# Attention and two MLPs on one core: product order, a planner rule, load order and four zero products

## The chip, the cores and the metric

One core of a Trainium2 chip runs the whole kernel. The metric is the device time of one launch in microseconds; of several runs the median is taken. TensorE is called PE here, VectorE DVE, ScalarE ACT, GpSimd POOL and SyncE SP, as in the profile.

## The reference

The kernel computes a decayed linear attention over 2 batches, 8 heads, 768 positions and a head size of 64, and then two MLPs over the 1536 tokens. Each MLP has a width of 512 and an inner width of 2048:

```python
for b in range(nb):                              # blocks of 64 positions
    intra = (q_b @ k_b.T) * Dmask @ v_b          # Dmask = lam ** (i - j) below the diagonal
    inter = (q_b * lam_pow) @ kv_state
    out[b] = intra + inter
    kv_state = lam_block * kv_state + (k_b * rev_pow).T @ v_b
x = out as [1536, 512]
h = x @ w_in;  x = (h * tanh(softplus(h))) @ w_out
h = x @ w2_in; y = relu(h) ** 2 @ w2_out
```

All arrays are float32.

## The kernel before

**Arithmetic.** Every float32 operand of an MLP product is split into a high and a low part in a reduced type (`fp32r`): ACT writes the high part, DVE subtracts it from the raw value for the low part. Each product is then three PE matmuls (`mm3`, L295): high by low, low by high, high by high. The weights arrive as int64 words; ACT (`m`, L565), DVE (`t`, L570) and a join on DVE (`bits`, L577) make float32 of them.

**Attention.** The tokens come in twelve chunks of 128. A call `attention(j)` handles chunks 2j and 2j+1: PE makes the scores (`sc`, L424, 16 matmuls a chunk), DVE multiplies them by the decay mask (`a`), POOL scales the keys (`kd`) and the queries (`qd`), PE makes the state's update (`sd`, L447), the output from the scores (`xo`, L466) and from the state (`xo`, L475). The two chunks of a call share one `xo` tile and one `sd` tile in PSUM. When a call's `xo` is complete, ACT and DVE read it: for the first 512 tokens into a high part (`xh`), a low part (`xl`) and a raw copy (`xr`), for the others into the raw copy alone. Each chunk needs two loads of 512 KB, `qk` and `kv`.

**MLPs.** Each of the two layers `L` goes through four blocks `g` of 512 inner columns. The tokens are three tiles of 512: tile 0 is handled apart, tiles 1 and 2 are a pair. The pair's products up and down are formed by seven products of sums and differences instead of eight (`up_pair`, `down_pair`): a product is two PE steps of 12 matmuls each (names `P1...`, `Q1...`), and results are passed on from one PSUM tile to the next by an ACT copy (`seed`, `keep`), which later products accumulate onto. Tile 0's up product is plain (`up`) in four blocks; in the blocks of `OWN`, (0,2), (1,1), (1,2) and (1,3), it is made by seven products as well (`up_own`): products U1, U7, U6, U2, U5, U4, U3 of 12 matmuls each. Their four accumulators a, b, f and e lie in two PSUM tiles of two banks: a and b in `ua`, f and e in `ub`. U1 goes to a, ACT copies a to b, U7 goes to f and is kept, U6 goes onto a, U2 onto b; ACT then copies a to e and DVE adds f to a; U5 goes onto e, U4 onto a, U3 onto e. Results a, b, e go through the activation into SBUF.

`TURNED` names the blocks (0,3) and (1,3), in which the pair's products come before those of tile 0, and the pair's down products before tile 0's. In the other blocks tile 0 comes first.

**The planner.** The order of every engine's instructions is written by a list scheduler in the kernel (`Plan`). Each step (`op`) has an engine, an estimated time, the values that it reads and writes, and for PE a `rank`. In the plan PE takes the ready step of the lowest rank; the other engines take the ready step whose due time (`late`) comes first, which follows from the PE steps that need it. Values live in 51 SBUF units of 4 KB a partition or in four PSUM tiles of two banks; a step is only taken when its values have a place. The first twelve loads on SP have their order from the list `FIRST`. The planner's times are estimates; on the chip semaphores hold each instruction until what it depends on is done. The planner knows a dependency between steps by their keys, which may name a half of a PSUM tile, such as `(one, 1)`.

**What follows the order.** The main loop at the end calls, for each block, the weights, `up` or `up_own`, the pair's `up_pair`, `down` and `down_pair`, with ranks that rise by 100 from call to call. Before the first load has landed PE runs eight zero matmuls (`warm_up`, L339) on a tile of its own.

Of the kernel before, what the change touches and what calls it, by code (L numbers as in the profile page):

```python
# [20 lines left out]
P = 128  # L21
# [3 lines left out]
CH = 128  # L25
TB = 512
WARM = 8
GF = 4
STRETCH = 1.4
SPLIT = ((0, 0),)  # L30
# [11 lines left out]
OWN = ((0, 2), (1, 1), (1, 2), (1, 3))  # L42
# [6 lines left out]
class Val:  # L49


    def __init__(self, name, space="S", dtype=F32):
        self.name, self.space, self.dtype = name, space, dtype
        self.left, self.slot, self.tile, self.was = 0, None, None, None
        self.full = self.seeded = False


class Op:
# [7 lines left out]
class Plan:  # L66
# [67 lines left out]
    def run(self, start, units):  # L134
        self.dues(start)
        free = {"S": list(range(units)), "P": list(range(4))}
        clock = dict.fromkeys(self.LAG, 0.0)
        left = {o: len(o.before) for o in self.ops}
        ready = {e: [] for e in self.LAG}
        for o in self.ops:  # L140
            if not left[o]:
                o.at = 0.0
                ready[o.eng].append(o)
        releases, order, last, table = [], [], {}, None

        turn = {}
        for o in sorted((o for o in self.ops if o.eng == "PE"), key=lambda o: o.rank):
            for v in o.vals:
                if v.space == "P":
                    turn.setdefault(v)  # L150

        def fits(v):


            if v.space == "S":
                return free["S"]
            full = [s for s in free["P"] if s in last and last[s].full]
            return full if v.seeded else [s for s in free["P"] if s not in full] + full

        front = sorted((o for o in self.ops if o.eng == "PE"), key=lambda o: o.rank)  # L160
        now, n, drift = 0.0, 0, 0.0
        while n < len(self.ops):
            while releases and releases[0][0] <= now:
                _, v = releases.pop(0)
                free[v.space].append(v.slot)
            while front and front[0].start is not None:
                drift = max(0.0, front[0].start - front[0].late)
                front.pop(0)
            for e in ready:
                if clock[e] > now:  # L170
                    continue
                can = [o for o in ready[e] if o.at <= now and (e == "PE" or o.late + drift - now < o.ahead)]
                if not can:
                    continue
                best = None
                for o in sorted(can, key=lambda o: o.rank if e == "PE" else o.late + (
                        self.SWITCH[1] if o.table and o.table != table else 0.0)):
                    need = defaultdict(int)
                    for v in o.vals:
                        if v.slot is None:  # L180
                            need[v.space] += 1
                    if any(v.seeded and v.slot is None and not fits(v) for v in o.vals):
                        continue
                    if o.eng != "PE" and need["P"] and next(v for v in turn if v.slot is None) not in o.vals:
                        continue
                    if all(len(free[s]) >= k + (o.spare if s == "S" else 0) for s, k in need.items()):
                        best = o
                        break
                if best is None:
                    continue  # L190
                o = best

                if e != "PE" and any(q.at > now and q.at < now + 0.7 * o.us and q.late < o.late - 2.0
                                     for q in ready[e]):
                    continue
                for v in sorted((v for v in o.vals if v.slot is None), key=lambda v: v.name):
                    v.slot = fits(v)[0]
                    free[v.space].remove(v.slot)
                    if v.space == "P":
                        last[v.slot] = v  # L200
                o.start, o.end = now, now + o.us
                if o.table and o.table != table:
                    o.end, table = o.end + self.SWITCH[0], o.table
                clock[e] = o.end
                ready[e].remove(o)
                order.append(o)
                n += 1
                for v in o.vals:
                    v.left -= 1
                    v.was = max(v.was or 0.0, o.end + o.lag)  # L210
                    if not v.left:
                        bisect.insort(releases, (v.was, v), key=lambda r: r[0])
                for a in o.after:
                    left[a] -= 1
                    if not left[a]:
                        a.at = max(b.end + (b.lag if (b.eng != a.eng or b.lag > 1) and (b, a) not in self.orders else 0.0)
                                   for b in a.before)
                        ready[a.eng].append(a)
            times = [c for c in clock.values() if c > now]
            times += [o.at for r in ready.values() for o in r if o.at > now]  # L220
            times += [r[0] for r in releases[:1]]
            times += [o.late + drift - o.ahead + 1e-6 for e in ready if e != "PE" for o in ready[e]
                      if o.late + drift - o.ahead + 1e-6 > now]
            times = [t for t in times if t > now]
            if not times:
                stuck = [o.name for r in ready.values() for o in r][:20]
                held = sorted({v.name for o in self.ops for v in o.vals if v.slot is not None and v.left and v.space == "S"})
                raise RuntimeError(f"stuck {held} at {now} with {n} of {len(self.ops)}: {stuck} {len(free['S'])} {len(free['P'])}")
            now = min(times)
        self.order = order  # L230
        return order
# [3 lines left out]
def attention_mlps(ctx, tc, lam, qk, kv, w_in, w_out, w2_in, w2_out, out):  # L235
# [21 lines left out]


    FIRST = {n: 0.01 * i for i, n in enumerate(
        "qk0 st00000 kv0 st00001 qk1 kv1 qk2 kv2 st00010 st00011 qk3 kv3".split())}  # L260

    plan = Plan({"DVE": AHEAD, "ACT": AHEAD, "POOL": AHEAD, "SP": AHEAD})
    op = plan.op
# [136 lines left out]
    def attention(j):  # L400
# [14 lines left out]
        for n, c in enumerate(cs):  # L415
# [7 lines left out]
                        r = slice(e * D, (e + 1) * D)  # L423
                        nc.tensor.matmul(out=o[:, e, p], lhsT=t[r, 1, p], rhs=t[r, 0, p], start=True, stop=True)  # L424

            op("PE", 0.95, scores, [(q, "q"), (q, "k")], [(sc, 0)], name=sc.name, rank=rank + n)
            op("DVE", 1.3, lambda a=a, sc=sc: tt(tl(a, 2, NP, CH), tl(sc, 2, NP, CH), tl(mask, 2, NP, CH), ALU.mult),
               [(sc, 0), *masked], [(a, 0)], name=a.name)
            if not (last and n):
# [268 lines left out]
                    pair.append(v)  # L698
                own[L, kind, n] = tuple(pair)

    def up_own(L, g, rank):

        w = 2 * CH
        back = g >= HOME[L]
# [21 lines left out]
        def product(i, o, onto):  # L726
            lh, ll, left = stationary(L, g, 0, i)
            rh, rl, right = moving(i)

            def products():  # L730
                for s in range(2):
                    c = slice(s * P, (s + 1) * P)
                    q = bank(o)[:, s * w : (s + 1) * w]
                    for k in range(2):
                        mm3(q, left(lh)[:, k, c], left(ll)[:, k, c], right(rh)[:, k], right(rl)[:, k],
                            s == 0 and k == 0, k == 1, onto=onto, pieces=True)

            parts = range(2) if back else x_parts(L, 0) if i < 4 else (0,)
            reads = [(lh, 0), (ll, 0), *((v, j) for v in (rh, rl) for j in parts)] + ([o] if onto else [])
            op("PE", 1.44, products, reads, [o], name=f"U{i}{L}{g}", rank=rank + count[0])  # L740
            count[0] += 1

        def to(x, y, name):
# [125 lines left out]
        n = {5: 0, 6: 1, 7: 2, 3: 3}[i]  # L869
        return s_hi[L, g, kind, n // 2], s_lo[L, g, kind, n // 2], lambda v: tl(v, 2, 2, 2 * P)[:, n % 2]  # L870

    def up_pair(L, g, rank, rest=None):

        count = [0]

        def product(i, o=None):
# [8 lines left out]
            for s in range(2):  # L885
# [4 lines left out]
                            k == 0, k == 1, onto=onto)  # L890

                reads = [(x, 0) for x in (lh, ll, rh, rl)] + ([(o, s)] if onto else [])
                op("PE", 1.37, products, reads, [(o, s)], name=f"P{i}{L}{g}{s}", rank=(rest if rest and count[0] > 1 else rank) + count[0])
                count[0] += 1
            return o

# [217 lines left out]
    def ranks(n=100):  # L1114
        nonlocal rank
        rank += n
        return rank

    for L in range(2):
        for g in range(NG):  # L1120
# [4 lines left out]
            if (L, g) == (1, 0):  # L1125
                own_forms(1)
            turned = (L, g) in TURNED
            first = turned and ranks()
            if (L, g) in OWN:
                sums(L, g)  # L1130
                up_own(L, g, ranks())
            else:
                up(L, g, 0, ranks() if rank else UP)
            weights(L, g, 1, 0)
# [11 lines left out]
            if (L, g) in SPLIT:  # L1146
                opened, before = before, ranks()
                up_pair(L, g, opened, ranks())
            else:
                up_pair(L, g, first or ranks())  # L1150
            sums(L, g, 1)
# [57 lines left out]
```

## Time and profile before

| | us |
|---|---|
| median of 3 runs | 541.66 (541.22 to 542.62) |
| the profiled execution | 542.34 |
| its span, first to last instruction | 539.3 |
| PE busy | 527.2 (98%), 3358 matmuls |
| DVE busy | 428.1 (79%) |
| ACT busy | 400.7 (74%) |
| POOL busy | 32.1 (6%) |
| HBM traffic | 88.08 MB read, 26.21 MB written, 212 GB/s over the span |

The span is divided into stages. Attention fills the first 62 us, mixed with the first block's up product; the blocks of layer 0 go to about 350 us with parts of layer 1 begun between, and those of layer 1 to the end. A busy PE is not PE at its peak: a matmul's row covers its way through the engine, and the next one starts before it ends. In the rows a line of many matmuls is merged (`x24`), with its start, its length and, in brackets, the idle time ahead of it with what ended it. Block (1,2)'s own products begin at 412.88 us, for instance.

### The profile page before, as it was taken

The page shows a single profiled execution, that of the slowest core. Times are in us where ns is not written, and L with a number is a line of the kernel's source. Part 1 is how long each engine was busy: PE and PEld are TensorE (multiplying, and loading weights), DVE is VectorE, ACT ScalarE, POOL GpSimd, SP SyncE. Part 2 cuts the span into 40 slices and gives each one's busy share as a digit, 9 for nine tenths or more (in the row PEclk, how much of TensorE's full clock was granted, in tenths as well). Part 3 has the DMA queues.
Part 4 walks back from the last instruction along what each step waited for, and adds up shares of the span by engine and source line. Part 5 has one row for each costly group of instructions (what it writes and reads, how often), then busy time and mean ns, then how long its engine had stood idle before and what let it go on. Part 6 is the DMA issues. An engine that isn't in the chain of part 4 may idle for free.

```text
span 539.3 us, 8479 instructions
## 1 busy us (share of the span) xinstructions
PE 527.2 (98%) x3358; PEld 457.0 (85%) x3358; DVE 428.1 (79%) x465; ACT 400.7 (74%) x460; POOL 32.1 (6%) x32
## 2 busy tenths in 40 slices
PE   8899999999999899999999999999999999999997
PEld 5798888888888788888888888998899888988995
DVE  5897977976996579889898989976886777887862
ACT  3667658876887879787888787868777878866930
POOL 2675200000000000000000000000000000000000
PEclk9999999999999999999999999999999999999999
DMA  8998330399489862954130400399899814970033
GB/s 314 409 408 276 120 116 1 117 369 400 167 326 409 278 198 99 384 218 157 37 121 1 153 4 1 134 359 414 340 354 363 314 62 152 404 302 1 1 118 117
DMA packets 33353, 114.84 MB, mean 213 GB/s; under 512 B 3618, under 2 KB 5666, under 8 KB 33314
## 3 DMA queue, kind: packets, MB, share of 16 engines
q1 hardware_dynamic: 33312, 114.31, 57.4%
q8 instruction: 26, 0.43, 0.3%
q14 instruction: 13, 0.11, 0.1%
q10 hardware_dynamic: 2, 0.00, 0.0%
HBM read 88.08 MB, written 26.21 MB: 212 GB/s over the span
## 4 chain that ended last, share of the span: by engine, by line
PE 96%; DVE 2%; ACT 1%; issue 0%; ACTq 0%
PE p L300 16%; PE dn L300 16%; PE q L300 13%; PE e L300 10%; PE o L300 9%; PE up L300 8%; PE b L300 8%; PE ua L300 4%; PE ub L300 3%; PE sc L424 2%; PE xo L466 2%; PE sd L447 1%; PE xo L475 1%; PE warm L339 1%; DVE a L291 1%; ACT ub L288 0%
## 5 line engine op out<-in xcount | busy, mean ns | idle before, releaser
L291 DVE TENSOR_TENSOR sl<-s,sh 128x1024 fp32r<-128x1024 f32 x32 | 40.6, 1275 | 10.1 <-ACT sh L288 10.0
L565 ACT ACTIVATE m<-st 128x512 f32<-128x512 f32 (+1 forms) x66 | 42.1, 666 | 6.7 <-DMA st<-in_moe_w_in_dram 6.5
L577 DVE SCALAR_TENSOR_TENSOR t<-m,t 128x1024 int32<-128x1024 int32 x32 | 38.6, 1221 | 6.1 <-ACT m L565 5.9
L291 DVE TENSOR_TENSOR wl<-t,wh 128x1024 fp32r<-128x1024 f32 x32 | 38.8, 1221 | 1.8 <-ACT wh L288 1.3
L291 DVE TENSOR_TENSOR el<-D,eh 128x1024 fp32r<-128x1024 f32 x32 | 38.9, 1219 | 1.6 <-ACT eh L288 0.7
L288 ACT ACTIVATE sh<-s 128x1024 fp32r<-128x1024 f32 x32 | 33.4, 1051 | 3.7 <-DVE s L291 3.7
L288 ACT ACTIVATE wh<-t 128x1024 fp32r<-128x1024 f32 x32 | 33.4, 1051 | 1.7 <-DVE t L577 1.7
L288 ACT ACTIVATE eh<-D 128x1024 fp32r<-128x1024 f32 x32 | 32.9, 1051 | 1.2 <-DVE D L291 1.2
L291 DVE TENSOR_TENSOR el<-h,eh 128x1024 fp32r<-128x1024 f32 x24 | 29.3, 1220 | 1.8 <-ACT eh L288 1.3
L570 DVE TENSOR_SCALAR t<-st 128x512 int32<-128x512 int32 (+1 forms) x66 | 27.1, 444 | 3.5 <-PE p L300 2.1
L288 ACT ACTIVATE ap<-o 128x1024 f32<-128x1024 f32 x18 | 18.5, 1027 | 12.8 <-PE o L300 12.8
L291 DVE TENSOR_TENSOR D<-h,h 128x1024 f32<-128x1024 f32 x16 | 19.1, 1222 | 8.8 <-ACT h L809 6.1
L291 DVE TENSOR_TENSOR gl<-h,gh 128x1024 fp32r<-128x1024 f32 x16 | 20.1, 1264 | 6.8 <-ACT gh L288 6.7
L288 ACT ACTIVATE eh<-h 128x1024 fp32r<-128x1024 f32 x24 | 25.1, 1053 | 0.2
L300 PE MATMUL p<-fl,wh 128*128 128x512 f32 x64 | 25.2, 393 | 0.0
L300 PE MATMUL p<-fh,wl 128*128 128x512 f32 x64 | 25.0, 390 | 0.0
L300 PE MATMUL dn<-wl,gh 128*128 128x512 f32 x64 | 24.9, 389 | 0.0
L300 PE MATMUL dn<-wh,gl 128*128 128x512 f32 x64 | 24.9, 389 | 0.0
L300 PE MATMUL p<-fh,wh 128*128 128x512 f32 x64 | 24.9, 389 | 0.0
L300 PE MATMUL dn<-gl,wh 128*128 128x512 f32 x64 | 24.9, 389 | 0.0
L300 PE MATMUL dn<-gh,wl 128*128 128x512 f32 x64 | 24.9, 389 | 0.0
L300 PE MATMUL dn<-gh,wh 128*128 128x512 f32 x64 | 24.9, 389 | 0.0
(261 smaller groups left out, 1742.3 us busy)
## 6 DMA issues: line engine op xcount, KB each, us to landing
st<-in_moe_w_out_dram SPq DMA_DIRECT2D x32, 512.0 KB, 6.6
fh<-f SPq DMA_DIRECT2D x28, 512.0 KB, 6.8
fl<-f SPq DMA_DIRECT2D x28, 512.0 KB, 6.3
st<-in_moe_w_in_dram SPq DMA_DIRECT2D x26, 512.0 KB, 6.1
f<-fh SPq DMA_DIRECT2D x14, 512.0 KB, 8.9
f<-fl SPq DMA_DIRECT2D x14, 512.0 KB, 8.5
qk<-in_qk_dram SPq DMA_DIRECT2D x12, 512.0 KB, 10.2
kv<-in_kv_dram SPq DMA_DIRECT2D x12, 512.0 KB, 10.2
```

The source lines that it names most:

```text
L288: nc.scalar.activation(out=o, in_=i, func=AF.Copy)
L291: nc.vector.tensor_tensor(out=o, in0=a, in1=b, op=alu)
L300: nc.tensor.matmul(out=out_, lhsT=a, rhs=b, start=start, stop=pieces or (last and i == 2), skip_group_check=not start if pieces else onto)
L339: nc.tensor.matmul(out=tl(warm)[:, 0], lhsT=z[:, 0:P], rhs=z, start=True, stop=True)
L424: nc.tensor.matmul(out=o[:, e, p], lhsT=t[r, 1, p], rhs=t[r, 0, p], start=True, stop=True)
L447: nc.tensor.matmul(out=o[e * D : (e + 1) * D, p], lhsT=t[:, p, 1 + e], rhs=t[:, p, 0 if e else 3], start=True, stop=True)
L466: nc.tensor.matmul(out=o[weighted(p, e), p, n], lhsT=v[:, p, 0 if e else 3], rhs=w[:, e, p], start=p % 2 == n == 0, stop=True, skip_group_ ...
L475: nc.tensor.matmul(out=o[weighted(h, e), h, n], lhsT=z[r, h], rhs=qd[r, h], start=False, stop=True, skip_group_check=True)
L565: nc.scalar.activation(out=tl(m)[o, i], in_=tl(st, TB, 2)[r, :, 1].bitcast(F32), func=AF.Prelu, scale=RANGE, alpha=BELOW)
L570: nc.vector.tensor_scalar(out=tl(t)[o, i], in0=tl(st, TB, 2)[r, :, 0], scalar1=29, scalar2=None, op0=ALU.logical_shift_right)
L577: nc.vector.scalar_tensor_tensor(out=tl(t), in0=tl(m).bitcast(I32), scalar=3, in1=tl(t), op0=ALU.logical_shift_left, op1=ALU.bitwise_or)
```

## The change

Four things are edited. (1) In the blocks of `OWN` the seven own products are given two ranks, and a product of the pair stands between the fourth (U2) and the fifth (U5): the pair's first product (P1) where tile 0 comes first, its last (P3) in the block (1,3), where the pair comes first. (2) The planner keeps, for every PSUM value, when each engine is done with it (`seen`), and does not take a step while another engine is still at a PSUM value of that step, whichever half. (3) The first twelve loads have another order: `qk1` is second, `kv2` tenth and the fourth rows of the first weights eleventh. (4) Four PE steps, each one zero matmul on the tile of `warm_up`, follow the scores of chunk 1.

```diff
+FILL = 4
 ...
 class Val:
         self.full = self.seeded = False
+        self.seen = {}
 ...
 class Plan:  def run
-        releases, order, last, table = [], [], {}, None
+        releases, order, last, table, halts = [], [], {}, None, []
 ...
                     if any(v.seeded and v.slot is None and not fits(v) for v in o.vals):
                         continue
+                    if any(t > now for v in o.vals if v.space == "P" for e_, t in v.seen.items() if e_ != e):
+                        continue
 ...
                 clock[e] = o.end
+                for v in o.vals:
+                    if v.space == "P":
+                        v.seen[e] = o.end + o.lag
+                        halts.append(o.end + o.lag)
 ...
+            halts = [t for t in halts if t > now]
+            times += halts
 ...
     FIRST = {n: 0.01 * i for i, n in enumerate(
-        "qk0 st00000 kv0 st00001 qk1 kv1 qk2 kv2 st00010 st00011 qk3 kv3".split())}
+        "qk0 qk1 st00000 kv0 st00001 kv1 st00010 qk2 qk3 kv2 st00011 kv3".split())}
 ...
-            op("PE", 0.95, scores, [(q, "q"), (q, "k")], [(sc, 0)], name=sc.name, rank=rank + n)
+            scored = op("PE", 0.95, scores, [(q, "q"), (q, "k")], [(sc, 0)], name=sc.name, rank=rank + n)
+            if c == 1:
+                for f in range(FILL):
+                    plan.follow(scored, op("PE", 0.45, lambda: warm_up(1), [(zval, 0)], [(warm, 0)], name="fill", rank=rank + 2 + f))
 ...
-    def up_own(L, g, rank):
+    def up_own(L, g, rank, rest):
 ...
-            op("PE", 1.44, products, reads, [o], name=f"U{i}{L}{g}", rank=rank + count[0])
+            op("PE", 1.44, products, reads, [o], name=f"U{i}{L}{g}", rank=(rank if count[0] < 4 else rest) + count[0])
 ...
-    def up_pair(L, g, rank, rest=None):
+    def up_pair(L, g, rank, rest=None, end=None):
 ...
-                op("PE", 1.37, products, reads, [(o, s)], name=f"P{i}{L}{g}{s}", rank=(rest if rest and count[0] > 1 else rank) + count[0])
+                op("PE", 1.37, products, reads, [(o, s)], name=f"P{i}{L}{g}{s}", rank=(end if end and count[0] > 11 else rest if rest and count[0] > 1 else rank) + count[0])
 ...
             first = turned and ranks()
+            if own_up:
+                start_own, between, rest_own = ranks(), ranks(), ranks()
             if (L, g) in OWN:
                 sums(L, g)
-                up_own(L, g, ranks())
+                up_own(L, g, start_own, rest_own)
 ...
+            elif own_up:
+                up_pair(L, g, *((first, first, between) if turned else (between, ranks())))
             else:
                 up_pair(L, g, first or ranks())
```

## Rows read from the trace of the kernel before

**Rows 1.** Table by stage: us, busy per engine, PEclk, DMA share, GB/s.
```profile
8.00:23.00 15.00, 11.93 (x177) 10.71 (x178) 11.78 (x16) 6.49 (x16) 8.06 (x7) 1.00 1.03 413
...
30.00:120.00 90.00, 90.00 (x778) 76.15 (x777) 75.37 (x78) 66.09 (x76) 19.54 (x16) 1.00 0.55 191
```

**Rows 2.** Waits of PE over the span: total us, times, longest.
```profile
PE ub L300 <- ACT ub L288: 2.9, 4, 0.7
PE up L300 <- ACT xr L288: 1.3, 1, 1.3
PE xo L466 <- DVE a L291: 1.3, 1, 1.3
...
PE ua L300 <- ACT h L756: 0.8, 1, 0.8
```

**Rows 3.** Chain of waits, block (1,2): start us, us, what.
```profile
415.92 2.89 PE ua L300 x24
...
419.53 1.69 PE ub L300 x12
421.22 1.44 PE ua L300 x12
```

**Rows 4.** Chain of waits, block (0,2).
```profile
172.87 2.89 PE ua L300 x24
...
180.66 1.44 PE ub L300 x12
```

**Rows 5.** Timeline of ACT, block (0,2): start us, us, instruction, idle before it.
```profile
175.84 0.58 ACT L288 ACTIVATE ub<-ua 128x512 f32<-128x512 f32 x1 [1.79 <-PE ua L300]
...
177.01 1.28 ACT L756 ACT_TABLE_LOAD   x1
...
184.88 1.01 ACT L288 ACTIVATE b<-p 128x1024 f32<-128x1024 f32 x1
```

**Rows 6.** Chain of waits, block (1,3).
```profile
490.55 2.72 PE e L300 x12
493.27 1.43 PE ua L300 x12
...
507.21 2.88 PE o L300 x24
```

**Rows 7.** Timeline, block (1,3), ACT and DVE.
```profile
493.31 1.03 ACT L820 ACTIVATE h<-e 128x1024 f32<-128x1024 f32 x1 [0.60 <-PE e L300]
...
503.22 2.52 DVE L291 TENSOR_TENSOR el<-D,eh 128x1024 fp32r<-128x1024 f32 x2
```

**Rows 8.** The load of line 411 issued at 2.6 us, and its landing.
```profile
L411 SPq DMA_DIRECT2D qk<-in_qk_dram x1: 500/500/500, 2.6 to 2.6; - x1
...
DMA to landing us min/median/max: 8.4/8.4/8.4
```

**Rows 9.** Timeline of PE in the start.
```profile
3.41 2.31 PE L339 MATMUL warm<-zero 128*128 128x512 bf16 x5
5.65 2.08 PE L424 MATMUL sc<-qk 64*128 64x128 f32 x16
9.06 1.98 PE L466 MATMUL xo<-a,kv 128*64 128x128 f32 x16 [1.33 <-DVE a L291]
...
11.82 3.69 PE L424 MATMUL sc<-qk 64*128 64x128 f32 x32
...
16.92 0.67 PE L475 MATMUL xo<-qk,state 64*64 64x128 f32 x16
...
20.34 1.16 PE L424 MATMUL sc<-qk 64*128 64x128 f32 x16 [0.67 <-DMA qk<-in_qk_dram]
22.85 0.39 PE L300 MATMUL up<-xh,wh 128*128 128x256 f32 x1 [1.34 <-ACT xr L288]
...
42.91 2.06 PE L424 MATMUL sc<-qk 64*128 64x128 f32 x32
```

**Rows 10.** Timeline of all engines in the start, DVE.
```profile
17.84 2.25 DVE L570 TENSOR_SCALAR t<-st 64x512 int32<-64x512 int32 x4
```

More of the change, by code (lines that the diff above doesn't have):

```diff
@@ L1127, in attention_mlps @@
             turned = (L, g) in TURNED
+            own_up = (L, g) in OWN
             first = turned and ranks()
+            if own_up:
+                start_own, between, rest_own = ranks(), ranks(), ranks()
             if (L, g) in OWN:
                 sums(L, g)
-                up_own(L, g, ranks())
+                up_own(L, g, start_own, rest_own)
             else:
```

## The prediction

> **What bounds the kernel now.** I read the table by stage first. From 30 to 120 us TensorE (PE) is busy 90.00 of 90.00 us; from 8 to 23 us only 11.93 of 15 [rows 1]. So a stage is worth what PE waits in it, and work moved between two PE products is free so long as its operands are there. The list of PE's waits then names every one of them: four times 0.7 us before a `ub` product, for ACT's copy; once 0.8 us before a `ua` product, for ACT; and three in the start: 1.3 before `up`, 1.3 before `xo` [rows 2], 0.7 before `sc`, the only one that names a load [rows 9]. The rest of the end is the last add and store, which the change leaves alone. So the change can gain in two places: the start, to 22.85 us, and the four blocks that take the first token tile by seven products (`up_own`).
>
> **The own blocks, before.** Block (1,2) stands for three. U6 and U2 begin at 415.92 and take 2.89, U5 would follow at 418.81 and U4 1.44 later, at 420.25; it begins at 421.22 [rows 3]. So one stall costs 0.97, more than the 0.73 shown as idle, as U5 fills the pipeline anew (1.69 for 1.44). In (0,2) U6 begins at 172.87 and U3 at 180.66; 2.89 + 2 x 1.44 would bring it at 178.64: 2.02, for there U4 waits too [rows 4]. Sum 3 x 0.97 + 2.02 = 4.93 us.
>
> Why it stalls: U5 accumulates onto a copy of U6's result. The copy started at 175.84, after 1.79 us idle, released by PE [rows 5]: not when U6 ended but when U2 had ended too, which writes the other half of the same PSUM tile. The order written by the planner put U2 ahead of the copy, since it knew no wait of a whole tile.
>
> [...] The row shows the wait, so the wait is of the tile, and the measurement decides.
>
> **The own blocks, after.** In (0,2), (1,1), (1,2) the pair's product 1 (two halves, 2.72 us as every pair product [rows 6]) is issued between U2 and U5; in (1,3), where the pair goes first, its last product, 3. No product is added. In those 2.72 us ACT needs 0.1 + at most 1.05 of something begun before + 0.58 for the copy: covered. In (0,2) a table load of 1.28 [rows 5] and Mish, a piece as long as the copy, come behind it, and they release U4, which is due 4.16 after U2: covered too. I take all 4.93 away. Bounds: 4.93 (nothing can go below no stall) to 1.0 (only (0,2)'s second wait goes).
>
> What it costs: product 1's accumulator is held for 3 x 1.44 us longer, as the third of four PSUM tiles; the fourth stays for product 7, and the copy `b`, which needs the next, comes when U4's tile is drained, as before. Loads: the form for product 1 is wanted some 6 us earlier; its two loads stand first of the fourteen in program order, and behind 20.34 us no wait of PE names a load [rows 2, 9]. Both 0 (bounds 0 to 1).
>
> In (1,3) product 3 moves behind four own products (5.8 us), while its result is the operand of the difference for down product 7. That product began at 507.21, product 3 ended at 493.27: 13.94 us [rows 6]. Afterwards it is 3 x 1.44 + 2.88 = 7.2. The chain in it (relu 1.03, square about as long, difference, copy, subtraction of about 1.2 each) is 5.6 us bare and some 6.1 with hand-overs, but before, unhurried, its first subtraction ended about 504.5, 11.2 behind product 3 [rows 7]. So the new wait lies between 0 and 4.0. ACT and DVE go by due time, so I take 0.5, near the low end.
>
> **The start, before.** The loads are 512 KB each and run back to back at 413 GB/s [rows 1]: 1.27 us a place. The second `qk` tile is fifth: issued at 2.6, landed 8.4 later, 11.0 [rows 8]; the fourth is eleventh, and the scores that wait for it start at 20.34 [rows 9], so 20.2. So place 2 lands at 7.2, 4 at 9.7, 6 at 12.3, 8 at 14.8, 9 at 16.1, 10 at 17.4. PE runs at the lower level: 16 scores take 2.08, the 32 from 11.82 take 3.69, later 32 take 2.06 [rows 9]. [...] Chunk 1's `xo` ends at 16.92 + 0.67 = 17.59; then ACT and DVE take turns on the same PSUM tile, DVE with 2.25 us of `t` work between [rows 10], and the first `up` product starts at 22.85 [rows 9]: 5.26 us.
>
> **The start, after.** `qk1` is second (7.2), so the scores of chunk 1 run straight behind those of chunk 0: 7.5 to 9.5. Then the four zero products: 5 `warm` take 2.31 [rows 9], pitch 0.43 at the lower level, so 1.7 us, to about 11.2. Chunk 0's values land fourth (9.7, was 8.4), so PE could go on at 9.8: the filling costs up to 1.4 us of path, or nothing where PE is already fast. [...] The x pieces take 5.26 less the 1.4 us that `t` stood in the way (third and fourth w_in rows now land at places 7 and 11): 3.8. [...] Chunks 2 and 3's scores run at 15 and 16.2; chunk 2's values land tenth (17.4, was 14.8), so its products end about 19.6. From there PE has all the work that it had at 22.85: 3.2 us won. What is late next: the fourth w_in rows, 20.2 for 17.4, whose splitting must be done when the first half of `up` runs out, some 28 us; 20.2 + 6 to 8 us of `t`, `m`, join, `wh`, `wl`. I take 0.5 off: 2.7 won. Bounds: 5.0 won (the three waits, 3.3, and 1.6 for the 32 slow scores) to 0.9 lost (the fourth rows' 2.8 us all on the path, less what stands between).
>
> [...]
>
> **The planner's new rule** (an instruction that touches a PSUM tile waits, in the plan, until other engines have left it) adds no instruction. It moves ACT's and DVE's order in the attention and own stages, and by later times everywhere. Both have idle time in the long stretch (DVE busy 75.4 of 90 us, ACT 66.1 [rows 1]) that hides it; 0, bounds 0.5 won to 1.5 lost.
>
> **Sum.** -4.93 + 0.5 - 2.7 = -7.1 us. The profiled execution took 542.34 (span 539.3 and 3.0 around it), which gives 535.2; the median of the runs lies 0.68 below it, so 541.66 - 7.1 = **534.5 us**.
>
> **Rivals.**
> 1. The start is bound by the loads, and nothing comes of it: 541.66 - 4.93 + 0.5 = 537.2. For it: every load slot is full, kv2 and the fourth rows come later. Against it: three waits before 23 us of which only 0.7 names a load [rows 2, 9].
> 2. The waits of the own blocks come back at (1,3), 4.0 for 0.5: 541.66 - 4.93 + 4.0 - 2.7 = 538.0. For it: 11.2 us before, 7.2 now. Against: before, nothing hurried it.
> 3. Slower: ACT's queue. Behind U3 the pair's copy `b` used to end at 185.89 [rows 5], 3.8 us behind U3's end (180.66 + 1.44 = 182.10 [rows 4]), where product 1 stood; now product 7 stands there and product 6 waits for that copy. If ACT keeps its order, each of three blocks loses 3.8 - 2.7 = 1.1, (1,3) 4.0, in all 7.3 against 4.93 won; the same queue cuts the x pieces, so the start gives 0: 541.66 + 2.4 = 544.0. It decides once the copy ends over 2.7 us behind U3. Against: before, the copy had no cause to come early, as a product stood in between.
> 4. The change does not do it: PE's plan finds product 1 not ready and the order stays, the start falls in the same places: 541.7.
>
> **How the numbers follow.** Forecast 0.50, rival 1 0.20, rival 2 0.12, rival 3 0.10, rival 4 0.08. 0.3% or 1.6 us is about what a measurement of this kernel can tell from no change. Faster by more (under 540.0): the first three less an edge of theirs, 0.78; within: 0.12; slower: 0.10. Low end of the range: both terms whole and half of what the start may give beyond, 532.0; high end 540.5, above rivals 1 and 2 and the low end of the own blocks' term.
>
> **What would show it.** In PE's waits the `ub` and `ua` rows are gone, and a `p` (in (1,3) an `e`) row of 12 products stands between `ua` x24 and `ub`. The first `up` product starts near 19.6, and the 32 scores no longer take 3.69. A wait of a `q` or `o` product for DVE at about 500 us is rival 2; of a `p` product for ACT `b` behind U3, rival 3; a PE gap at 24 to 30 us, before `up`, is rival 1. If `ub` still waits for its copy, the reading of the tile's wait was wrong.

## The result and the profile after

| | before | after |
|---|---|---|
| median of 4 runs each, us | 542.14 (541.22 to 543.08) | 535.15 (534.92 to 537.86) |
| ratio | | 0.9882, 95% interval 0.9845 to 0.9919 |
| the profiled execution, us | 542.34 | 534.95 |
| its span, us | 539.3 | 532.9 |
| first down product of block (0,0) begins | 63.76 | 62.09 |
| from there to the end of the span | 475.54 | 470.81 |

Faster by 7.0 us, forecast 7.1. The last two lines divide the span at a point where the start's work is done: 1.67 us come from the start (forecast 2.7) and 4.73 from what follows, the own blocks (forecast 4.93 less 0.5). That is 6.4. The remaining 0.95 of the two profiled executions lies outside the span: 3.04 us around it before, 2.05 after. In the runs of the kernel before that accompany the experiments it is 2.1 at the median, so the 3.04 was one execution's accident. That the medians lie 7.0 apart where 7.1 was forecast is in part luck: of the two terms one came out larger than forecast, the other smaller, and together they give 6.4.

Waits of PE over the span, after (total us, times, longest), against [rows 2]:

```profile
PE warm L349 <- DVE zero L359: 1.2, 1, 1.2
PE xo L479 <- DMA kv<-in_kv_dram: 0.9, 1, 0.9
PE sd L460 <- POOL kv L443: 0.6, 1, 0.6
PE sc L434 <- PE sc L434: 0.3, 1, 0.3
```

The five waits of the own blocks are gone, and so are those for `xr` and `a`. What is left belongs to the start. The table by stage, against [rows 1]:

```profile
8.00:23.00 15.00, 13.16 (x216) 10.30 (x214) 13.44 (x16) 10.38 (x24) 10.19 (x8) 1.00 1.03 413
30.00:120.00 90.00, 89.70 (x766) 75.37 (x765) 76.56 (x82) 66.28 (x75) 16.44 (x15) 1.00 0.55 197
```

PE misses 1.84 us of the start's 15, where it missed 3.07. But 0.30 is now missing between 30 and 120 us, where nothing was: the `sc` row above, to which "What ate the start's lead" returns.

Block (1,2) in the chain of waits, against [rows 3]:

```profile
411.50 2.88 PE ua L310 x24
414.38 2.75 PE p L310 x12
417.12 1.43 PE ub L310 x12
418.56 1.44 PE ua L310 x12
```

From U6 to U4 it took 5.30 us; now it takes 7.06 with a pair product of 2.75 inside, so 4.31 of its own: 0.99 less, and U5, with no wait ahead of it, takes 1.43 for 1.69. ACT in block (0,2), against [rows 5]:

```profile
174.21 0.58 ACT L298 ACTIVATE ub<-ua 128x512 f32<-128x512 f32 x1 [0.84 <-PE ua L310]
174.81 1.28 ACT L769 ACT_TABLE_LOAD   x1
...
182.74 1.01 ACT L298 ACTIVATE b<-p 128x1024 f32<-128x1024 f32 x1
```

The copy still waits until PE has left the whole tile (U6 and U2 run from 171.23 to 174.11, the copy starts at 174.21); it is PE that now has something else to do. The pair's copy `b`, on which rival 3 hung, ends at 183.75, and the pair's product 6 did wait for it. Timeline of PE's weight loads:

```profile
183.80 0.19 PEld L310 LDWEIGHTS p<-fl,sh 128*128 128x128 f32 x1 [0.29 <-ACT b L298]
```

Block (1,3), chain of waits against [rows 6]:

```profile
490.92 2.75 PE e L310 x12
493.67 1.43 PE ub L310 x12
...
500.86 2.88 PE o L310 x24
```

and the operand of that `o` product on ACT and DVE, against [rows 7]:

```profile
493.70 1.03 ACT L833 ACTIVATE h<-e 128x1024 f32<-128x1024 f32 x1 [0.65 <-PE e L310]
```

```profile
499.39 1.22 DVE L301 TENSOR_TENSOR el<-D,eh 128x1024 fp32r<-128x1024 f32 x1
```

From the end of product 3 to product 7 there are 7.19 us, as computed (7.2). This subtraction ends at 500.61, 0.25 before the `o` piece of the chain: just in time.

The start, timeline of PE against [rows 9]:

```profile
5.65 3.39 PE L434 MATMUL sc<-qk 64*128 64x128 f32 x32
8.97 1.04 PE L349 MATMUL warm<-zero 128*128 128x512 bf16 x4
...
13.38 0.67 PE L488 MATMUL xo<-qk,state 64*64 64x128 f32 x16
...
18.25 1.09 PE L479 MATMUL xo<-a,kv 128*64 128x128 f32 x16 [0.89 <-DMA kv<-in_kv_dram]
...
20.49 0.39 PE L310 MATMUL up<-xh,wh 128*128 128x256 f32 x1
```

and of DVE between chunk 1 and `up`:

```profile
15.33 1.22 DVE L301 TENSOR_TENSOR wl<-t,wh 128x1024 fp32r<-128x1024 f32 x1
16.47 2.35 DVE L301 TENSOR_TENSOR a<-sc,mask 128x1024 f32<-128x1024 f32 x2
18.73 1.28 DVE L301 TENSOR_TENSOR xl<-xo,xh 128x512 fp32r<-128x512 f32 x2
```

Chunk 1 ends at 14.05 (17.59 before). `up` begins 6.44 us later, not 3.8: the `t` work of [rows 10] is out of the way, but a weight's low part and the masks of chunks 2 and 3 stand there instead, 3.57 us for 2.25, and PE has put chunk 2's products first, which wait for `kv2`.

### The profile page after: what moved, and what is told of

Same layout as the page of the kernel before. It is cut to its first block, busy times and chain, and to the rows that moved or that the text cites. A ratio compares the mean times of both kernels' runs of the same rounds, so it can differ in the third digit from the quotient of the medians.

```text
span 532.9 us, 8493 instructions
## 1 busy us (share of the span) xinstructions
PE 525.7 (99%) x3362; PEld 455.1 (85%) x3362; DVE 427.9 (80%) x465; ACT 403.0 (76%) x462; POOL 31.1 (6%) x32
## 3 DMA queue, kind: packets, MB, share of 16 engines
q1 hardware_dynamic: 33312, 114.31, 57.9%
## 4 chain that ended last, share of the span: by engine, by line
PE 96%; DMA 2%; SPq 1%; issue 0%; DVE 0%
PE p L310 16%; PE dn L310 16%; PE q L310 14%; PE e L310 10%; PE o L310 9%; PE up L310 8%; PE b L310 8%; PE ua L310 4%; PE ub L310 3%; DMA kv<-in_kv_dram 2%; PE xo L479 2%; PE sc L434 2%; PE xo L488 1%; PE sd L460 1%; SPq L421 0%; SPq L571 0%
## 5 line engine op out<-in xcount | busy, mean ns | idle before, releaser
L301 DVE TENSOR_TENSOR sl<-s,sh 128x1024 fp32r<-128x1024 f32 x32 | 39.5, 1247 | 6.5 <-ACT sh L298 6.2
L583 DVE TENSOR_SCALAR t<-st 128x512 int32<-128x512 int32 (+1 forms) x66 | 28.4, 465 | 1.0 <-DMA st<-in_moe_w_in_dram 0.9
L310 PE MATMUL p<-fl,sh 128*128 128x512 f32 x64 | 25.1, 392 | 0.0
L310 PE MATMUL p<-fh,sl 128*128 128x512 f32 x64 | 25.0, 390 | 0.0
L310 PE MATMUL e<-fl,sh 128*128 128x512 f32 x64 | 24.9, 389 | 0.0
```

What stands on the lines that cost most here:

```text
L301: nc.vector.tensor_tensor(out=o, in0=a, in1=b, op=alu)
L310: nc.tensor.matmul(out=out_, lhsT=a, rhs=b, start=start, stop=pieces or (last and i == 2), skip_group_check=not start if pieces else onto)
L583: nc.vector.tensor_scalar(out=tl(t)[o, i], in0=tl(st, TB, 2)[r, :, 0], scalar1=29, scalar2=None, op0=ALU.logical_shift_right)
```

## The experiments

Each kernel is one edit away from the kernel before, from the changed kernel, or from an earlier experiment. All were timed beside the kernel before. "Start" is the time of the first down product of block (0,0), "rest" the span from there, both from the profiled execution; the start of one kernel differs between executions (the spans of the kernel before ran from 537.9 to 540.7 us), while the rest of kernels with the same order there differs little (475.51 to 475.57 with the old own blocks). So starts that are a microsecond apart in two profiles can be the same.

| kernel | rule | ranks | load order | zero products | start | rest | median, before | ratio, 95% |
|---|---|---|---|---|---|---|---|---|
| before | | | | | 63.76 | 475.54 | | 1 |
| `own` | | x | | | 62.96 | 472.44 | 538.59, 541.07 | 0.9946 [0.9926, 0.9966] |
| `seen` | x | | | | 63.02 | 471.78 | 536.95, 541.07 | 0.9918 [0.9896, 0.9940] |
| `loads` | | | x | | 62.79 | 475.51 | 540.59, 541.07 | 0.9982 [0.9966, 0.9997] |
| `fill` | | | | x | 64.03 | 475.57 | 541.65, 541.07 | 1.0009 [0.9995, 1.0022] |
| `again` | x | x | x | x | 62.75 | 470.85 | 535.78, 542.25 | 0.9886 [0.9864, 0.9907] |
| `no_fill` | x | x | x | | 62.62 | 470.88 | 535.91, 542.25 | 0.9890 [0.9869, 0.9911] |
| `no_loads` | x | x | | x | 67.41 | 470.89 | 539.76, 542.25 | 0.9955 [0.9935, 0.9974] |
| `kv_early` | x | x | other | x | 62.54 | 470.86 | 535.34, 542.25 | 0.9876 [0.9862, 0.9890] |
| `no_own` | x | | x | x | 62.35 | 470.65 | 534.73, 540.88 | 0.9883 [0.9864, 0.9902] |
| `no_seen` | | x | x | x | 64.05 | 471.15 | 536.88, 540.88 | 0.9922 [0.9907, 0.9938] |
| `late_in` | x | x | other | x | 61.72 | 470.78 | 534.55, 540.88 | 0.9881 [0.9864, 0.9897] |
| `late_all` | x | x | x | x | 63.22 | 470.78 | 534.32, 542.42 | 0.9862 [0.9836, 0.9887] |

### One part alone

**`own`**, the ranks of the own and pair products alone:

```diff
-                up_own(L, g, ranks())
+                up_own(L, g, start_own, rest_own)
...
+            elif own_up:
+                up_pair(L, g, *((first, first, between) if turned else (between, ranks())))
```

> Only the order of the own blocks is changed: a product of the pair between U2 and U5, in all four blocks; planner, loads and start as before. Theory (the 4.93 us are PE's wait for a copy, and any product of 2.72 us put in front covers it): the four ub waits and the ua wait are gone, the start is unchanged (first up product at 22.8), the time falls by 4.7 to 5.0 us, ratio 0.991. Rival (the planner must know the tile's wait for the order to fall right): at least two of the five waits stay, gain 1 to 3 us, and new waits of a p or b product for ACT's copy show.

Measured: 3.10 us of the rest, not all; one wait of the five stayed, less than the rival asked for. In block (1,1) the planner, which knows no wait here, took the pair's product early, between U1 and U7, so that it was spent when U5 needed cover. Chain of waits of `own`:

```profile
351.21 2.75 PE p L300 x12
353.96 1.43 PE ub L300 x12
355.39 2.89 PE ua L300 x24
...
358.37 0.59 ACT ub L288
358.96 0.04 issue
359.00 1.70 PE ub L300 x12
```

A rank only says which step is preferred when several are ready; it does not hold a product back.

**`seen`**, the planner's rule alone:

```diff
+                    if any(t > now for v in o.vals if v.space == "P" for e_, t in v.seen.items() if e_ != e):
+                        continue
```

> Only the planner's rule on PSUM tiles is added. Theory: it adds no instruction and mends no wait by itself, since no product stands ready by rank to be put into the gap: the ub waits stay (3 to 4 of 0.7 us), the first up product starts 0 to 1.5 us earlier because xh and xr are read in one row instead of in turns with DVE; time -1.5 to +0.5 us. Rival (the rule carries the start's gain): the first up product starts at 20.5 and the time falls by 1.6 us or more. Second rival: PE, blocked in the plan, takes a later product by itself in the own blocks; then the ub waits are gone here too and the time falls by over 3 us.

Measured: 3.76 us of the rest, more than the ranks give, with no own wait left: the second rival. Once PE's next own product is blocked in the plan, PE takes the next ready one of higher rank by itself. Two new waits of pair products stand in the profile, 0.4 us for DVE (`fl`) and 0.2 for ACT's copy `b`, part of what is missing to 4.73. Chain of waits of `seen`, block (0,2):

```profile
172.14 2.88 PE ua L309 x24
175.02 1.39 PE p L309 x6
176.41 1.43 PE ub L309 x12
177.84 1.39 PE p L309 x6
179.23 1.43 PE ub L309 x12
```

So the step "the planner's new rule: 0" fell with this run: the rule alone makes most of the own blocks' gain.

**`loads`**, the new order of the first twelve loads alone:

```diff
-        "qk0 st00000 kv0 st00001 qk1 kv1 qk2 kv2 st00010 st00011 qk3 kv3".split())}
+        "qk0 qk1 st00000 kv0 st00001 kv1 st00010 qk2 qk3 kv2 st00011 kv3".split())}
```

> Only the order of the first twelve loads is changed. Theory (the start is bound by the loads and by what PE can do with them): the scores of chunk 1 follow those of chunk 0 at 7.5 us, the equal point of the start comes 1 to 2 us earlier, the waits of the own blocks stay; time -1 to -2 us. Rival (the later place of chunk 2's values and of the fourth weight rows costs what the second place of qk1 gives): 0 to +1.5 us.

Measured: 0.2%, with an interval from 0.03 to 0.34%. The scores of chunk 1 do run earlier, and PE then waits. Timeline of PE in `loads`:

```profile
10.38 1.09 PE L466 MATMUL xo<-a,kv 128*64 128x128 f32 x16 [2.23 <-DVE t L570]
```

The row names DVE's `t`, which these products do not read. Their masks were done at 9.95, and their values, `kv0`, landed at 10.24, 0.14 us ahead of them. In `again` the same products begin at 10.56, 0.13 behind `kv0`. So the wait is for the load, as are the next ones of `xo` in `loads` (2.0 us in all for `kv`).

**`fill`**, the four zero products alone:

```diff
+            if c == 1:
+                for f in range(FILL):
+                    plan.follow(scored, op("PE", 0.45, lambda: warm_up(1), [(zval, 0)], [(warm, 0)], name="fill", rank=rank + 2 + f))
```

> Only the four zero products are added, behind the scores of chunk 1, which here run at about 12 us. Theory: PE is busy there already, so they add 4 x 0.43 = 1.7 us of PE time at the lower level to the start, partly hidden by the wait for chunk 1's mask product; time 0 to +1.7 us. [...]

Measured: no difference that can be told.

### The changed kernel with one part undone

**`again`** is the changed kernel once more, as the measure for its neighbours.

> The changed kernel once more, beside the others of this call. Expected: 534.5 to 536, 5.5 to 6.5 us under the kernel before; no wait of PE for ACT in the own blocks; its down products of the first block begin at 62.0 to 62.3 us.

Measured: 535.78, 6.5 us under the kernel before, as expected; the down products at 62.75, later than expected.

**`no_fill`** leaves the four zero products out:

```diff
-                    plan.follow(scored, op("PE", 0.45, lambda: warm_up(1), [(zval, 0)], [(warm, 0)], name="fill", rank=rank + 2 + f))
```

> The changed kernel without its four zero products. [...] Theory B (they only fill a wait for chunk 0's values): 0, within 0.3 us, and xo of chunk 0 still starts at 9.8 to 9.9. Theory C (they hold PE up): -0.3 to -1.3 us.

Measured: 535.91 beside 535.78 on the same chip. Slow products are in the profile (chunk 0's `xo` begins at 10.93, after 2.11 us idle, and takes 1.53 us, chunk 1's 1.75; in `again` both take 1.09), but the time does not show them. In these two profiles `up` begins 1.0 us later without the zero products, as `kv2` landed 1.0 later, and `again` then lost its lead in a wait that `no_fill` has not (the scores of chunk 11, below). The zero products are worth nothing here, and nothing alone.

**`no_loads`** has the old load order:

```diff
-        "qk0 qk1 st00000 kv0 st00001 kv1 st00010 qk2 qk3 kv2 st00011 kv3".split())}
+        "qk0 st00000 kv0 st00001 qk1 kv1 qk2 kv2 st00010 st00011 qk3 kv3".split())}
```

> The changed kernel with the old order of the first twelve loads; the zero products then stand behind the scores of chunk 1 at 12 us. Theory (the load order carries the start's gain): the down products of the first block begin at 63.3 to 64, +1.3 to +2 us against the changed kernel; the own blocks stay without waits. Rival (the planner's rule carries it): within 0.5 us of the changed kernel.

Measured: 4.0 us slower than `again`, more than the theory asked for. The rest is the same; the start is lost, and 3.65 us worse than before the change in the profiled execution, the slowest of six (some 2.3 by the median spans, 537.7 and 540.0, less the rests). The second wait in these rows belongs to "What ate the start's lead". Timeline of PE in `no_loads`:

```profile
21.10 1.09 PE L479 MATMUL xo<-a,kv 128*64 128x128 f32 x16 [2.34 <-DVE a L301]
...
51.52 0.37 PE L434 MATMUL sc<-qk 64*128 64x128 f32 x1
53.22 1.16 PE L434 MATMUL sc<-qk 64*128 64x128 f32 x15 [1.32 <-issue]
```

The masks come late here. But this is not the rule with the old load order alone: `seen` has both, and its start is 63.02. What `no_loads` has besides are the ranks and the zero products. The ranks change no engine's order ahead of block (0,2), neither in `own` against the kernel before nor in `again` against `no_own`. So the zero products are left: with them the scores of chunk 2 run at 16.98, behind chunk 1's products, where in `seen` they run at 13.33, ahead of them. That they are the cause is not shown, since no run has the rule, the old load order and the zero products alone.

**`no_own`** has the old ranks:

```diff
-                up_own(L, g, start_own, rest_own)
+                up_own(L, g, ranks())
...
-            elif own_up:
-                up_pair(L, g, *((first, first, between) if turned else (between, ranks())))
```

> The changed kernel without the new ranks of the own and pair products: planner's rule, load order and zero products stay. If the rule alone leaves PE with small gaps and switches in the own blocks, as it did by itself (471.78 us from the first down products to the end, against 470.85 with both), the time is 0.9 above the changed kernel: 536.4. If the ranks add nothing once the rule is there: 535.6, and 470.9 from the down products to the end. No wait of a ub product in either case.

Measured: 534.73, a rest of 470.65. The second theory holds: with the rule in the plan, and the loads and zero products beside it, the ranks add nothing.

**`no_seen`** has no rule:

```diff
-                    if any(t > now for v in o.vals if v.space == "P" for e_, t in v.seen.items() if e_ != e):
-                        continue
```

> The changed kernel without the planner's rule: ranks, load order and zero products stay. Own blocks as with the ranks alone: 472.44 us from the first down products to the end, one wait of 0.7 before ub in block (1,1). For the start two theories. The load order brings its gain by itself: down products at 62.1 to 62.8, 537.0 to 537.8. The load order brings it only with the rule, since ACT and DVE else take the weight pieces first (as in the run of the load order alone, with waits of xo for DVE t of 2.2): down products at 63 or later, 538.0 or more.

Measured: 536.88. The ranks by themselves remove all five waits here (the rest is 471.15, and PE's waits have no `ub` row), where in `own` one stayed: the other start moved the planner off the early product in (1,1). So 472.44 was wrong. The start is 1.70 us behind `no_own` on the same chip, and by the medians, less the rests, 1.65. That would be the second theory, but the profiles do not show it: up to the first `up` product PE's order is the same in both, and the whole 1.63 us by which `up` begins later (22.08 for 20.45) is that by which `kv2` landed later (19.71 for 18.08). And `loads`, which has no rule either, starts early: its median span is 537.8 us, 538.9 for the kernel before on the same chip, which less its rest makes the start 62.3, between the changed kernel's 62.09 and 62.75. Whether the load order needs the rule stays open.

### What ate the start's lead

At the end of the first block's `up` products the changed kernel was 2.22 us ahead of before (35.95 for 38.17), at the down products 1.67.

**`kv_early`** puts `kv2` and `qk3` ahead of the third weight rows:

```diff
-        "qk0 qk1 st00000 kv0 st00001 kv1 st00010 qk2 qk3 kv2 st00011 kv3".split())}
+        "qk0 qk1 st00000 kv0 st00001 kv1 qk2 kv2 qk3 st00010 kv3 st00011".split())}
```

> The changed kernel with another load order: chunk 2's values eighth instead of tenth, the third weight rows tenth. Theory (in the changed kernel the start hangs on the landing of chunk 2's values at 18.1 us, behind which xo waits 0.9 us): that wait goes, xo of chunk 2 starts at 16 to 17.5, the first up product at 19.5 to 20, time -0.5 to -1.2 us. Rival (the weight rows are late next, or ACT and DVE reading the x pieces): a wait of up for DVE or ACT takes its place, time -0.3 to +1 us.

Measured: `up` begins at 19.56 (20.49 after) and ends 0.65 us earlier (35.30), but the down products begin at 62.54, no better. The lead is gone at the scores of chunk 11. Timeline of PE in `kv_early`:

```profile
51.96 1.16 PE L434 MATMUL sc<-qk 64*128 64x128 f32 x16
54.51 1.16 PE L434 MATMUL sc<-qk 64*128 64x128 f32 x16 [1.39 <-issue]
```

No engine and no load released them; the profile calls it issue. In `no_loads` such a wait splits one chunk's sixteen matmuls after the first (above); the second matmul's record holds no wait for a semaphore at all. So PE's instructions themselves may have been missing. Two rows of the page after, PE's from the busy times and queue q8's from the queues (packets, MB):

```profile
PE 525.7 (99%) x3362; PEld 455.1 (85%) x3362; DVE 427.9 (80%) x465; ACT 403.0 (76%) x462; POOL 31.1 (6%) x32
...
q8 instruction: 26, 0.43, 0.3%
```

0.43 MB over 3362 matmuls and 3362 weight loads is 64 bytes each: q8 brings PE's program, 16 KB or 256 instructions a packet. PE's instructions begun when the packet at about 50 us started, counted in the trace, PE's wait behind it, and the time from the end of `up` to the down products:

| kernel | packet | PE instructions begun | wait before chunk 11 | `up` to down |
|---|---|---|---|---|
| before | 51.69 to 53.01 | 1308 | none | 25.59 |
| after | 51.23 to 52.59 | 1385 | 0.29 | 26.14 |
| `no_own` | 51.51 to 52.75 | 1397 | 0.57 | 26.43 |
| `again` | 51.85 to 53.20 | 1404 | 0.84 | 26.70 |
| `kv_early` | 52.02 to 53.21 | 1444 | 1.39 | 27.24 |

The further PE was ahead of the packet, the longer it stood. PE gave out at 1472 or 1473 in the four that waited and at 1216 in `no_loads`, 256 apart: one packet. In all five it went on 1.2 to 1.6 us behind the packet's end. And the last column gives the lead back whole: 26.14 less 25.59 is the 0.55 us between 2.22 and 1.67. Two runs moved what lies in the packet's way, the second halves of the weight rows of block (0,1), four transfers of 256 KB.

**`late_in`**, on `kv_early`:

```diff
-            op("SP", 1.3, load, [], [(st, 0)], name=st.name, due=FIRST.get(st.name), spare=SPARE[0])
+            op("SP", 1.3, load, [], [(st, 0)], name=st.name, due=FIRST.get(st.name), spare=SPARE[0], ahead=35 if (L, g, kind) == (0, 1, 0) and k >= 2 else None)
```

> The kernel of kv_early with one edit: the second half of the weight rows of block (0,1), four transfers of 256 KB on 64 partitions that landed between 52 and 54 us, is taken up by the plan up to 20 us later. They are wanted only after 90 us. Theory A (TensorE's own instructions, fetched in packets of 16 KB by the same DMA engines, come late behind these transfers: in kv_early a packet that was due at about 48.5 moved from 52.02 to 53.21, and the scores of chunk 11 began at 54.51 after 1.39 us without a releaser): if they land behind 56 us, the packet moves near 49 to 50, the wait before the scores of chunk 11 is under 0.3, the first block's down products begin at 61.2 to 61.6 instead of 62.54, and the time is 534.0 to 534.5. Theory B (the scores wait for something of the attention stage itself, a PSUM tile or their loads): the wait of 1.4 us stays, down products at 62.5, 535.3. If the four transfers land as before, the run says nothing.

Measured: the four landed between 51.84 and 55.95, none behind 56 as the expectation asked. But they were issued from 47.69 on, in `kv_early` from 40.10, and between 46.5 and 51 us the data took 53.2% of the engines instead of 101.9%. The packet went from 48.71 to 49.82, with 1252 instructions begun, and the scores of chunks 10 and 11 ran as one row without a wait; down products at 61.72, 25.58 behind the end of `up`.

**`late_all`**, the same edit on the changed kernel, further:

```diff
+..., spare=SPARE[0], ahead=22 if (L, g, kind) == (0, 1, 0) and k >= 2 else None)
```

> The changed kernel with one edit, as in late_in but further: the four half-width transfers of block (0,1) are taken up only behind three transfers of down weights, which were issued after 58 us, so none of them lies before 56 us this time. Theory A (TensorE's instruction packets come late behind these transfers): the packet that went at 51.2 to 51.9 in two profiles of the changed kernel goes at 48.5 to 49.5, and no wait stands before the scores of chunk 11 (0.29 and 0.84 there); the down products begin 0.3 to 0.8 earlier than without the edit, at 61.4 to 62.0, and the time is 534.3 to 534.9, if the transfers, now wanted some 40 us after they land, hold nothing else up. Theory B (the scores wait for something of the attention stage): the wait stays between 0.3 and 0.9 and the time at 535.2 to 535.8. Theory C (late_in owed its time to its slower start alone, PE arriving later): the packet goes at 51 to 52 again.

Measured: the four landed behind 71 us. The profiled execution was the slowest of four (536.02; the others 534.01 to 534.46), its start itself late: the masks of chunks 2 and 3 came a microsecond later. So the packet, at 50.13, missed the time expected, but not the place: 1249 instructions begun. And no wait followed (`up` to down 25.59). Theory B falls, and so does C, for the packet left when PE was as far as in `late_in`, though later. Queues between 46.5 and 51 us (packets, MB, share of 16 engines), after:

```profile
q1 hardware_dynamic: 305, 1.01, 100.5%
q14 instruction: 1, 0.01, 0.6%
```

and in `late_all`:

```profile
q1 hardware_dynamic: 127, 0.44, 24.4%
q8 instruction: 1, 0.02, 1.4%
q14 instruction: 2, 0.02, 1.2%
```

With the data at 100.5% of the engines no packet of PE's program got through in these 4.5 us; with it at 24.4% one did. By the medians `late_all` and `late_in` are the fastest of all. But `late_in` (ratio 0.9881) is no better than `kv_early`, on which it stands (0.9876), and the interval of `late_all` (0.9862) overlaps that of `again` (0.9886): that the whole kernel gets faster without the wait is not shown.

## Why the prediction was right, point by point

**The own blocks, -4.93: right.** By block, from the distance of their first products to the first down product: 1.80 in (0,2), 0.97 in (1,1) and in (1,2), the remainder, 0.97, in (1,3); 4.71 in all. The lower value of (0,2), 0.22 under the forecast, is in the pair's products: the 36 matmuls behind U2 take 8.41 us in three pieces, where they took 8.19 in one, since the plan put half of product 7 between U5 and U4; behind U3 the other half alone did not quite cover the copy `b`. The wait is of the tile: the copy was still released only when U2 had ended (174.11, the copy at 174.21).

**The new wait in (1,3), 0.5: 0.** The window was 7.19 us and the chain filled it to the last 0.25. Rival 2 fell: hurried, ACT and DVE took 6.9 us from product 3 to the first subtraction, where they had taken 11.2 unhurried.

**ACT's queue: rival 3 fell by its size.** `b` ended 1.2 us behind U3's end (182.55), where 2.7 would have decided with a whole product there. With half of one in (0,2), its mechanism shows: product 6's weight load waited 0.29 us for the copy (0.30 in `again`). In (1,1) and (1,2) `b` ended 0.8 behind U3, ahead of a whole product's end.

**The rule, 0: wrong in what it does, right in the sum.** I costed it as a mover of ACT and DVE and gave the gain to the ranks. The runs show the gain twice: `seen` alone takes 3.76 of 4.7, `no_own` all of it without the ranks. The step that failed is the list of what the rule moves: PE obeys it too. What the rule does in the start is not shown (`no_loads`, `no_seen`).

**The start, -2.7: mis-sized.** -1.67 in the profiled execution, -1.0 in `again`, inside the bounds. Chunk 1 ended 3.54 earlier than before (14.05 for 17.59); the term "the x pieces take 3.8" measured 6.44, for I took `t` out of DVE's way and did not ask what the plan would put there. The 3.2 won rested on chunk 2's products, to end at 19.6; they ended at 20.49, 2.36 ahead of 22.85, since `kv2` landed at 18.11 for 17.4. Of this 2.22 was left at the end of `up`, with no gap for the fourth weight rows, for which I had taken 0.5 off. Then 0.55 (1.11 in `again`) went to the late packet, which no view of before could show: PE got there too late to notice. PE was fast behind the zero products in this execution (chunk 0's `xo` took 1.09 us, 1.98 before), and the scores of chunks 2 and 3, forecast at 15 and 16.2, ran from 14.92 on (2.44 us for the 32); that the zero products make PE fast no run shows: without them the same `xo` took 1.53 in `no_fill`, but 1.09 in `own`. What was missing lay with `kv2` and the packet.

**Rival 1** (the loads bind) is partly true: the one `xo` wait names `kv2`, and in `again`, `no_own` and `no_seen` two or three `xo` products wait for a `kv` load, 1.6 to 3.9 us in all. `kv_early` freed the one of `kv2`, and the time stayed.

## What to carry to other kernels

Give a planner the waits that the trace shows, here of a whole PSUM tile (0.7 us, four times), before ordering products by hand: the rule alone found most of the cover that the ranks spelled out, and the ranks without it could be spent too early. When work leaves an engine's way, look up what the order puts there next. And undo each part by itself, in more than one company, before giving it a gain: the new load order is worth 0.2% alone and 4 us in the changed kernel, and the 4 us do not belong to it and the rule alone, since `seen`, with the old order, does not lose them.

## What the runs showed of the hardware

**PE's program shares the DMA engines with the data.** As above: in `after` queue q8 brought it in 26 packets, 0.3% of the 16 engines' span beside 57.9% for the data of q1. With the data at 101.9% of the engines a packet of 256 instructions started up to 195 instructions late (`kv_early`, 1444 for 1249), and PE, on scores that take 1.16 us a chunk, ran dry for 0.18 (`no_seen`) to 1.39 us (`kv_early`). With the data at 53.2% (`late_in`) and 24.4% (`late_all`) the packet started at 1252 and 1249.

**PE's faster pace sets in at other times in executions of the same order.** In `own` the order of PE's instructions is that of before up to the first own block. Timeline of PE in `own`:

```profile
8.94 1.09 PE L466 MATMUL xo<-a,kv 128*64 128x128 f32 x16 [1.33 <-DVE a L291]
```

The same sixteen matmuls took 1.98 us before [rows 9], so here PE was at its faster pace by 9 us and there still at the slower, though the granted clock reads 1.00 for both, and in both PE had stood for 1.33 us just before. The down products came 0.80 us earlier, with PE's order unchanged; how much of that the pace gave is not shown.
